# Linear attention, gated convolution and channel mixing on one core: heating transposes, query and first weights put in another order

## The chip, the cores and the metric

The kernel runs on one core of a Trainium2 chip. Times are device microseconds (us) of one execution; the number compared is the median of several runs. One execution was taken with the hardware profiler, and all rows below are from it. Of the engines, PE is TensorE, PEld its weight load, DVE VectorE, ACT ScalarE, POOL GpSimd, and SP issues most transfers.

## The reference

Three layers follow each other on batch 8, sequence 576, width 512 (8 heads of 64); the weights come as 64-bit numbers, q, k and v as 32-bit ones.

```python
# attention: softmax of q over the head's width, of k over the sequence
q_s = exp(q - max(q, -1)); q_s /= sum(q_s, -1) + 1e-9
k_s = exp(k - max(k, 2));  k_s /= sum(k_s, 2) + 1e-9
x = q_s @ (k_s^T @ v)                       # per batch and head, heads put side by side
# gated convolution
gate = sigmoid(sum_t conv_w[t] * x shifted by 4 - t)      # 5 taps, per channel
x = (gate * (x @ w_val)) @ w_out
# channel mixing, x_prev = x one step earlier
xk = mu_k * x + (1 - mu_k) * x_prev;  xr = mu_r * x + (1 - mu_r) * x_prev
out = sigmoid(xr @ w_r) * (relu(xk @ w_k) ** 2 @ w_v)     # w_k 512x1024, w_v 1024x512
```

## The kernel before, in words

The 4608 tokens are worked in 12 tiles of 384. Each tile goes through the same steps: query's softmax (qexp, qnorm), its transposes (xturn: tile pq) and copies (xq: tile q), the product with the attention matrix (x: tile px, copied to xf), the gate (taps on DVE at L705, tanh on ACT at L714), the product with W_val (V: pv), gf = gate times pv, the product with W_out (Y: py), mixing with the token before (y, mixk: yf and xm), then W_r (R: racc), W_k (H: ph) and W_v (A: vacc).

The attention matrix of a batch is made in rounds of 4 heads from k and v. A round takes k's maximum over the sequence: DVE over the steps (tile pm), PE turns it (pmT, L359), DVE takes the maximum m (L362), PE spreads it (mx, L405), DVE subtracts it from k (L406), ACT takes the exponential (L409), PE multiplies with v (kvacc, L419), and DVE divides (kvf, L431). Query's first tile comes in two halves of 4 heads, tile came, each with its own maximum, exponential (L492) and division (L503).

Weights come as 64-bit numbers (tile raw) and are decoded to 32 bits (tile whole) by ACT and DVE (L165 to L178). Raw weights pass through six buffers; five of them (LEFT_WEIGHTS: wval1, wr0, wk1, wk2, wk5) share a single seventh one, so that each of their loads waits for the decode of the one before. The transfers stand in SP's queue one behind another.

`heat` (L925) is a group of 8 transposes of the identity into a bank that nobody reads.

Three things set the order. FRONT, a table of step names, is the order in which the steps of the first tiles are written; up to the step START a scheduler may then move instructions. `after(key)` says that an instruction is to stand behind another one, named by `latest`. BEHIND does the same for the decoding of a weight: ("mus", "m1.0") puts its part on ACT behind the step that left mus, and its part on DVE behind the maximum of round 0.

Of the kernel before, what the change touches and what calls it, by code (L numbers as in the profile page):

```python
# [77 lines left out]
def tile_linear_attention_gated_conv_channel_mix(  # L78
# [61 lines left out]
    def f32(ap):  # L140
        return ap.bitcast(F32)
# [212 lines left out]
    def kv_turn(st):  # L354
        pm, n, x = st["pm"], HR * D // P, rounds.index(st)
        pmT = bank_of(st, "pmT", 1)
        with after("matmul" if x > 1 else None):
            for j in range(n):
                nc.tensor.transpose(pmT[:, j * P:(j + 1) * P], pm[:, j * P:(j + 1) * P], f32(ident))  # L359
        m1 = odd.tile([P, n], F32, tag="m1", bufs=2, name="m1")  # L360
        with after("kvf.0" if x == 1 else None):
            latest[f"m1.{x}"] = nc.vector.tensor_reduce(  # L362
                out=m1, in_=pmT[:, :n * P].rearrange("p (j t) -> p j t", j=n), axis=AX.X, op=ALU.max
            )
        st["m1"] = m1
# [45 lines left out]
    def kv_mm(st):  # L411
# [4 lines left out]
        for x in range(n):  # L416
            for s in range(NST):
                for e in range(2):
                    nc.tensor.matmul(  # L419
                        acc[e * D:(e + 1) * D, x * VW:(x + 1) * VW], lhsT=kt[:, 2 * x + e, s, :],  # L420
                        rhs=st["v"][:, 2 * x + e, s, :], start=(s == 0), stop=(s == NST - 1),
                    )
# [185 lines left out]
    def x_turn(st, i, c):  # L608
        qt = st["qt"]
        pq = ps_t.tile([P, 512], F32, tag="t", name="pq")  # L610
        for t in range(NT):
            nc.tensor.transpose(  # L612
                pq[:, t * P:(t + 1) * P], qt[:, t, 2 * c:2 * c + 2, :].rearrange("p h d -> p (h d)"), f32(ident)
            )
        st["pq", c] = pq
# [75 lines left out]
    def x_gate(st, i, c):  # L691
# [10 lines left out]
        with after("kexp.1" if i == 0 and c == 0 else None):  # L702
            nc.scalar.activation(gx(gate), data, AF.Copy, scale=tap(c, HALO))  # L703
        for sh in range(1, NTAP):
            latest[f"tap.{sh}"] = nc.vector.scalar_tensor_tensor(  # L705
                out=gx(gate), in0=xv[:, :, HALO - sh:HALO - sh + L], scalar=tap(c, HALO - sh),
                in1=gx(gate), op0=ALU.mult, op1=ALU.add,
            )
# [11 lines left out]
    def main_steps(i, xs):  # L720
# [63 lines left out]
        def keep_y(c, py):  # L784
            yv = padded(i, 1, "yf", 4, "yf")
            fill_past(i, yv, tail_y[:, c:c + 1])
            latest["yf"] = nc.scalar.activation(yv[:, :, 1:], gx(py[:, :T]), AF.Copy, scale=0.5 if i == 0 else 1.0)
            keep_tail(i, yv, tail_y[:, c:c + 1])
            st["yv", c] = yv
            mix(c, "xr", mur, omr, "x", x_pair)  # L790

        def mix(c, key, mu, om, tag, pair):
            yv = st["yv", c]
            xf = one(tag, 8, "xm") if i == 0 else scratch("xm")
            nc.scalar.activation(gx(xf), yv[:, :, 0:L], AF.Copy, scale=om[:, c:c + 1])  # L795
# [129 lines left out]
    def heat():  # L925

        po = ps_acc.tile([P, 512], F32, tag="acc", name="heat")
        for x in range(8):
            nc.tensor.transpose(po[:, x % 4 * P:(x % 4 + 1) * P], f32(ident), f32(ident))  # L929
# [76 lines left out]
```

## Time and profile before

| | |
|---|---|
| median of 3 runs | 802.05 us (801.37 to 802.36) |
| profiled execution, its own time | 801.24 us |
| its span from first to last instruction | 799.4 us |
| PE busy, PEld busy | 782.9 us (98%), 688.6 us (86%) |
| DVE busy, ACT busy | 598.2 us (75%), 481.9 us (60%) |
| mean granted clock of PE | 0.994 |
| W_k's loads, 512 KB each | 8, median 3.2 us from issue to landing |

The shares are of the whole span. In slices of 20 us (40 of them) PE is busy 5 tenths of the first one and 8 of the second, and 9 or more from then on; the granted clock is 8 tenths in the first and 9 in the others. So the page alone says little about the front, and the rows below are from views with narrow windows there. A duration is that of one instruction from its start to its modelled end; matmuls overlap, so two starts tell more of the pace than one duration. In the timeline one fp32 matmul of a product is counted twice (x2), a transpose once.

### The profile page before, as it was taken

How to read it: one execution, taken by the hardware profiler on the slowest of the kernel's cores; microseconds unless marked ns; L12 is line 12 of the kernel's file. 1: busy time of each engine (PE TensorE's matmuls, PEld its weight loads, DVE VectorE, ACT ScalarE, POOL GpSimd, SP SyncE). 2: the span in 40 equal slices, each digit the busy share in tenths (PEclk: the TensorE clock that was granted, in tenths of full speed). 3: DMA queues.
4: the chain of work that ended last, by engine and by line, in shares of the span. 5: the costliest groups of instructions: out<-in, count | busy, mean ns of one | idle time of the engine just before them, and what ended most of it. 6: DMA issues, size and time to landing. Idle time of an engine off the chain costs nothing.

```text
span 799.4 us, 12507 instructions
## 1 busy us (share of the span) xinstructions
PE 782.9 (98%) x4426; PEld 688.6 (86%) x4426; DVE 598.2 (75%) x1182; ACT 481.9 (60%) x977; POOL 64.4 (8%) x224
## 2 busy tenths in 40 slices
PE   5899999999999999999999999999999999999998
PEld 5545569989989999999999999999999998998996
DVE  5799879988788588687888768768878857755511
ACT  3678477745763763763773773673674665574542
POOL 2012010100001110100010200100000100110000
PEclk8999999999999999999999999999999999999999
DMA  9788220033332412411531501502513112110001
GB/s 324 203 247 276 64 80 1 6 102 104 82 100 75 111 40 67 119 40 53 140 90 57 139 25 62 139 5 80 137 44 108 57 30 69 57 36 28 12 1 40
DMA packets 91709, 68.89 MB, mean 86 GB/s; under 512 B 48738, under 2 KB 83454, under 8 KB 91646
## 3 DMA queue, kind: packets, MB, share of 16 engines
q1 hardware_dynamic: 91600, 68.06, 28.5%
q8 instruction: 35, 0.57, 0.3%
q14 instruction: 28, 0.23, 0.1%
q10 hardware_dynamic: 46, 0.02, 0.0%
HBM read 51.54 MB, written 16.53 MB: 85 GB/s over the span
## 4 chain that ended last, share of the span: by engine, by line
PE 90%; DVE 4%; DMA 2%; ACT 2%; issue 1%; DVEq 0%; ACTq 0%
PE vacc L585 24%; PE ph L585 24%; PE py L585 12%; PE pv L585 11%; PE racc L585 11%; PE px L585 3%; PE kvacc L419 2%; DVE whole L176 1%; DMA raw<-in_moe_w_k_dram 1%; DMA raw<-in_moe_w_v_dram 1%; PE heat L929 1%; DMA kt<-in_k_dram 1%; ACT raw L169 1%; DVE gate L705 1%; PE pq L612 1%
## 5 line engine op out<-in xcount | busy, mean ns | idle before, releaser
L705 DVE SCALAR_TENSOR_TENSOR gate<-xf,cw,gate 128x384 f32<-128x384 f32 x192 | 116.7, 615 | 5.7 <-ACT gate L703 2.4
L585 PE MATMUL ph<-xkh,wk_hi 128*128 128x384 f32 x352 | 118.5, 337 | 0.0
L585 PE MATMUL ph<-xkl,wk_hi 128*128 128x384 f32 x352 | 118.2, 336 | 0.0
L585 PE MATMUL ph<-xkh,lower 128*128 128x384 f32 x352 | 117.8, 336 | 0.0
L822 ACT ACTIVATE rf<-ph 128x384 f32<-128x384 f32 x96 | 46.9, 489 | 96.2 <-PE ph L585 95.8
L578 DVE TENSOR_TENSOR kl<-rf,kh 128x384 fp32r<-128x384 f32 x88 | 49.0, 556 | 74.5 <-ACT kh L577 74.2
L585 PE MATMUL vacc<-wv_hi,kh 128*128 128x512 f32 x264 | 103.9, 394 | 0.0
L585 PE MATMUL vacc<-lower,kh 128*128 128x512 f32 x264 | 103.4, 392 | 0.0
L585 PE MATMUL vacc<-wv_hi,kl 128*128 128x512 f32 x264 | 103.2, 392 | 0.0
L577 ACT CAST gh<-gf 128x384 fp32r<-128x384 f32 x44 | 22.6, 513 | 104.2 <-DVE gf L757 104.2
L585 PEld LDWEIGHTS ph<-xkh,wk_hi 128*128 128x128 f32 x352 | 66.1, 188 | 2.4 <-ACT xkh L577 0.2
L585 PEld LDWEIGHTS ph<-xkh,lower 128*128 128x128 f32 x352 | 66.1, 188 | 2.3
L585 PEld LDWEIGHTS ph<-xkl,wk_hi 128*128 128x128 f32 x352 | 66.1, 188 | 0.0
L796 DVE SCALAR_TENSOR_TENSOR xm<-yf,mus,xm 128x384 f32<-128x384 f32 x96 | 56.1, 612 | 12.8 <-ACT xm L795 12.5
L585 PE MATMUL py<-gh,wout_hi 128*128 128x384 f32 x176 | 60.0, 341 | 0.0
L585 PE MATMUL pv<-xh,wval_hi 128*128 128x384 f32 x176 | 59.3, 337 | 0.0
L585 PE MATMUL py<-gl,wout_hi 128*128 128x384 f32 x176 | 58.9, 337 | 0.0
L585 PE MATMUL pv<-xl,wval_hi 128*128 128x384 f32 x176 | 58.9, 335 | 0.0
L585 PE MATMUL pv<-xh,lower 128*128 128x384 f32 x176 | 58.9, 334 | 0.0
L585 PEld LDWEIGHTS vacc<-wv_hi,kl 128*128 128x128 f32 x264 | 49.5, 188 | 10.8 <-DVE kl L578 0.3
L585 PE MATMUL py<-gh,lower 128*128 128x384 f32 x176 | 58.8, 336 | 0.0
L795 ACT ACTIVATE xm<-yf,mus 128x384 f32<-128x384 f32 x96 | 56.4, 615 | 3.0 <-DVE xrl L578 1.6
(153 smaller groups left out, 1703.1 us busy)
## 6 DMA issues: line engine op xcount, KB each, us to landing
out_dram<-rs SPq DMA_DIRECT2D x36, 256.0 KB, 2.3
kt<-in_k_dram SPq DMA_DIRECT2D x16, 512.0 KB, 4.3
vt<-in_v_dram SPq DMA_DIRECT2D x56, 128.0 KB, 4.0
turned<-sq SPq DMA_DIRECT2D x36, 192.0 KB, 2.1
qT<-turned SPq DMA_DIRECT2D x72, 96.0 KB, 2.2
qn<-in_q_dram SPq DMA_DIRECT2D x24, 192.0 KB, 3.5
raw<-in_moe_w_k_dram SPq DMA_DIRECT2D x8, 512.0 KB, 3.2
raw<-in_moe_w_v_dram SPq DMA_DIRECT2D x8, 512.0 KB, 3.3
```

What stands on the lines that cost most here:

```text
L169: nc.scalar.activation(f32(high), f32(high), AF.Prelu, scale=2.0 ** -112, alpha=2.0 ** 32)
L176: return nc.vector.scalar_tensor_tensor(out=out.bitcast(U32), in0=high, scalar=3, in1=low, op0=ALU.logical_shift_left, op1=ALU.bitwise_or)
L419: nc.tensor.matmul(acc[e * D:(e + 1) * D, x * VW:(x + 1) * VW], lhsT=kt[:, 2 * x + e, s, :], rhs=st["v"][:, 2 * x + e, s, :], start=(s == ...
L577: latest["round"] = nc.scalar.copy(pair[0], a)
L578: latest["split"] = nc.vector.tensor_sub(pair[1], a, f32(pair[0]))
L585: latest["matmul"] = nc.tensor.matmul(po, lhsT=left[a], rhs=right[b], start=start and x == 0, stop=stop and x == len(m) - 1)
L612: nc.tensor.transpose(pq[:, t * P:(t + 1) * P], qt[:, t, 2 * c:2 * c + 2, :].rearrange("p h d -> p (h d)"), f32(ident))
L705: latest[f"tap.{sh}"] = nc.vector.scalar_tensor_tensor(out=gx(gate), in0=xv[:, :, HALO - sh:HALO - sh + L], scalar=tap(c, HALO - sh), in1= ...
L795: nc.scalar.activation(gx(xf), yv[:, :, 0:L], AF.Copy, scale=om[:, c:c + 1])
L796: latest["mix"] = nc.vector.scalar_tensor_tensor(out=gx(xf), in0=yv[:, :, 1:], scalar=mu[:, c:c + 1], in1=gx(xf), op0=ALU.mult, op1=ALU.add)
L822: nc.scalar.activation(rf, ph[:, :T], AF.Relu)
L929: nc.tensor.transpose(po[:, x % 4 * P:(x % 4 + 1) * P], f32(ident), f32(ident))
```

## The change

The table FRONT is written anew: heat6 and heat3 stand ahead of mm0 (the first kvacc), heat0 behind xturn1.0, heat7 is gone, and turn1 (the second pmT) stands behind query's first two turns. New places for `after`: the first kvacc behind the heats; the second pmT behind the heats; a group of heats behind pq of chunk 1 once that is there; in the first tile, ACT's part of gate 1 behind the exponential of query's second half, and the gates' third and fourth taps behind the division of it (qmul). The decoding of wval2 and wval3 on DVE goes behind that division (before: behind kvf of round 1), and that of wk0, wk1, wv0 and wv1 behind the mixing steps (before: wv0 alone, and its part on ACT behind yf).

```diff
@@ -22,10 +22,10 @@
 
 FRONT = (
     "qload.0 qload0.0 lk0 cload consts lwval0 lv0 lk1 lwval1 lv1 lwval2 qload1.0 lwval3 lwout0 lwout1 lwr0 max0 turn0 "
-    "exp0 lwout3 lwr1 heat1 heat2 lwout2 qexp0.0 wval0 vcopy0 mm0 heat6 qnorm0.0 heat3 heat0 heat7 max1 turn1 xturn0.0 "
-    "xq0.0 xturn1.0 xq1.0 x0.0 exp1 wval1 x1.0 vcopy1 others qexp1.0 V0.0 mm1 qnorm1.0 gate0.0 V1.0 xturn2.0 xq2.0 "
+    "exp0 lwout3 lwr1 heat1 heat2 lwout2 qexp0.0 wval0 vcopy0 heat6 heat3 mm0 qnorm0.0 max1 xturn0.0 xq0.0 xturn1.0 "
+    "xq1.0 heat0 turn1 x0.0 exp1 wval1 x1.0 vcopy1 others qexp1.0 V0.0 mm1 qnorm1.0 gate0.0 V1.0 xturn2.0 xq2.0 "
     "x2.0 wval2 wval3 V2.0 xturn3.0 xq3.0 x3.0 gate1.0 gate2.0 V3.0 lwr2 wout0 gf0.0 gf1.0 gate3.0 gf2.0 lwk1 gf3.0 "
-    "lwk2 lwr3 wout1 lwk0 wout2 wout3 Y0.0 wr0 Y1.0 wr1 Y2.0 wr2 Y3.0 lwv1 y0.0 wk1 y1.0 max2 y2.0 y3.0 lwv0 wk0 lwk3 "
+    "lwk2 lwr3 wout1 lwk0 wout2 wout3 Y0.0 wr0 Y1.0 wr1 Y2.0 wr2 Y3.0 lwv1 y0.0 y1.0 max2 y2.0 y3.0 wk1 lwv0 wk0 lwk3 "
     "lwk5 R0.0 R1.0 lwk4 lwk7 wr3 mixk0.0 lwk6 mixk1.0 R2.0 mixk2.0 R3.0 mixk3.0 wk3 wk2 turn2 exp2 lwv2 qload.1 H0.0 "
     "wv1 lwv5 H1.0 H2.0 wk4 lwv4 wv0 mm2 wk5 rsig.0 A0.0 lwv3 H3.0 wk6 wv5 max3 A1.0 wk7 H4.0 wv2 qexp.1 turn3 exp3 "
     "A2.0 wv3 H5.0 lwv6 lwv7 mm3 qnorm.1 xturn0.1 xq0.1 wv7 A3.0 wv4 H6.0 x0.1 xturn1.1 xq1.1 gate0.1 A4.0 x1.1 "
@@ -65,10 +65,10 @@
 
 ON_SCALAR = "wval0 wval1 wval2 wval3 wout0 wout1 wout2 wout3".split()
 BEHIND = {
-    "wval0": ("mus", "m1.0"), "wval1": ("kexp.0", "m1.1"), "wval2": ("qexp.1", "kvf.1"), "wval3": ("qexp.1", "kvf.1"),
+    "wval0": ("mus", "m1.0"), "wval1": ("kexp.0", "m1.1"), "wval2": ("qexp.1", "qmul"), "wval3": ("qexp.1", "qmul"),
     "wout0": ("xf.3", "kvf.1"), "wout1": ("xf.3", "kvf.1"), "wout2": ("xf.3", "gf.1"), "wout3": ("xf.3", "gf.1"),
     "wr0": ("tanh", "gf.1"), "wr1": ("tanh", "gf.1"), "wr2": ("tanh", "gf.1"), "wr3": ("tanh", "gf.1"),
-    "wv0": ("yf", "mix"),
+    "wk0": ("part", "mix"), "wk1": ("part", "mix"), "wv0": ("part", "mix"), "wv1": ("part", "mix"),
 }
 
 LEFT_WEIGHTS = "wval1 wr0 wk1 wk2 wk5".split()
@@ -354,7 +354,7 @@
     def kv_turn(st):
         pm, n, x = st["pm"], HR * D // P, rounds.index(st)
         pmT = bank_of(st, "pmT", 1)
-        with after("matmul" if x > 1 else None):
+        with after((None, "heat", "matmul", "matmul")[x] if x < 4 else "matmul"):
             for j in range(n):
                 nc.tensor.transpose(pmT[:, j * P:(j + 1) * P], pm[:, j * P:(j + 1) * P], f32(ident))
         m1 = odd.tile([P, n], F32, tag="m1", bufs=2, name="m1")
@@ -416,10 +416,11 @@
         for x in range(n):
             for s in range(NST):
                 for e in range(2):
-                    nc.tensor.matmul(
-                        acc[e * D:(e + 1) * D, x * VW:(x + 1) * VW], lhsT=kt[:, 2 * x + e, s, :],
-                        rhs=st["v"][:, 2 * x + e, s, :], start=(s == 0), stop=(s == NST - 1),
-                    )
+                    with after("heat" if st is rounds[0] and x + s + e == 0 else None):
+                        nc.tensor.matmul(
+                            acc[e * D:(e + 1) * D, x * VW:(x + 1) * VW], lhsT=kt[:, 2 * x + e, s, :],
+                            rhs=st["v"][:, 2 * x + e, s, :], start=(s == 0), stop=(s == NST - 1),
+                        )
         sums = acc[:, 0:n * VW].rearrange("p (j c) -> p j c", c=VW)
         den = odd.tile([P, n], F32, tag="den", bufs=2, name="den")
         d3 = den.rearrange("p (j o) -> p j o", o=1)
@@ -609,7 +610,7 @@
         qt = st["qt"]
         pq = ps_t.tile([P, 512], F32, tag="t", name="pq")
         for t in range(NT):
-            nc.tensor.transpose(
+            latest[f"pq.{c}"] = nc.tensor.transpose(
                 pq[:, t * P:(t + 1) * P], qt[:, t, 2 * c:2 * c + 2, :].rearrange("p h d -> p (h d)"), f32(ident)
             )
         st["pq", c] = pq
@@ -699,13 +700,14 @@
         if i == 0 and c in CONV_ON_TENSOR:
             nc.scalar.activation(gate, conv_on_tensor(xv, c), AF.Tanh, scale=0.5)
             return
-        with after("kexp.1" if i == 0 and c == 0 else None):
+        with after(("kexp.1", "qexp.1", None, None)[c] if i == 0 else None):
             nc.scalar.activation(gx(gate), data, AF.Copy, scale=tap(c, HALO))
         for sh in range(1, NTAP):
-            latest[f"tap.{sh}"] = nc.vector.scalar_tensor_tensor(
-                out=gx(gate), in0=xv[:, :, HALO - sh:HALO - sh + L], scalar=tap(c, HALO - sh),
-                in1=gx(gate), op0=ALU.mult, op1=ALU.add,
-            )
+            with after("qmul" if i == 0 and sh > 2 else None):
+                latest[f"tap.{sh}"] = nc.vector.scalar_tensor_tensor(
+                    out=gx(gate), in0=xv[:, :, HALO - sh:HALO - sh + L], scalar=tap(c, HALO - sh),
+                    in1=gx(gate), op0=ALU.mult, op1=ALU.add,
+                )
         if i < LATER or c < 2:
             x_tanh(st, c)
 
@@ -784,7 +786,7 @@
         def keep_y(c, py):
             yv = padded(i, 1, "yf", 4, "yf")
             fill_past(i, yv, tail_y[:, c:c + 1])
-            latest["yf"] = nc.scalar.activation(yv[:, :, 1:], gx(py[:, :T]), AF.Copy, scale=0.5 if i == 0 else 1.0)
+            nc.scalar.activation(yv[:, :, 1:], gx(py[:, :T]), AF.Copy, scale=0.5 if i == 0 else 1.0)
             keep_tail(i, yv, tail_y[:, c:c + 1])
             st["yv", c] = yv
             mix(c, "xr", mur, omr, "x", x_pair)
@@ -792,7 +794,7 @@
         def mix(c, key, mu, om, tag, pair):
             yv = st["yv", c]
             xf = one(tag, 8, "xm") if i == 0 else scratch("xm")
-            nc.scalar.activation(gx(xf), yv[:, :, 0:L], AF.Copy, scale=om[:, c:c + 1])
+            latest["part"] = nc.scalar.activation(gx(xf), yv[:, :, 0:L], AF.Copy, scale=om[:, c:c + 1])
             latest["mix"] = nc.vector.scalar_tensor_tensor(
                 out=gx(xf), in0=yv[:, :, 1:], scalar=mu[:, c:c + 1], in1=gx(xf), op0=ALU.mult, op1=ALU.add
             )
@@ -926,7 +928,8 @@
 
         po = ps_acc.tile([P, 512], F32, tag="acc", name="heat")
         for x in range(8):
-            nc.tensor.transpose(po[:, x % 4 * P:(x % 4 + 1) * P], f32(ident), f32(ident))
+            with after("pq.1" if "pq.1" in latest and x == 0 else None):
+                latest["heat"] = nc.tensor.transpose(po[:, x % 4 * P:(x % 4 + 1) * P], f32(ident), f32(ident))
 
     acts = [{} for _ in range(NB + 1)]
     todo_front = {"cload": load_consts, "consts": turn_consts, "others": other_consts, "kvsplit": kv_split}
```

PE's instructions, from the heats ahead of the first pmT to the first pv. Before:

```order
L929 MATMUL heat<-ident 128x128 x14
L359 MATMUL pmT<-ident,pm 128x128 x2
L405 MATMUL mx<-ident,m_187 128x128 x2
L419 MATMUL kvacc<-vt,kt 64x65 x20
L929 MATMUL heat<-ident 128x128 x32
L359 MATMUL pmT<-ident,pm 128x128 x2
L612 MATMUL pq<-ident,qt 128x128 x6
L585 MATMUL px<-q,kvf_118 128x384
L405 MATMUL mx<-ident,m_302 128x128 x2
L585 MATMUL px<-q,kvf_118 128x384
L585 MATMUL pv<-xf,whole 128x384 x4
```

The same place on PE now:

```order
L932 MATMUL heat<-ident 128x128 x15
L359 MATMUL pmT<-ident,pm 128x128 x2
L932 MATMUL heat<-ident 128x128 x5
L405 MATMUL mx<-ident,m_187 128x128 x2
L932 MATMUL heat<-ident 128x128 x10
L420 MATMUL kvacc<-vt,kt 64x65 x20
L613 MATMUL pq<-ident,qt 128x128 x6
L932 MATMUL heat<-ident 128x128 x8
L359 MATMUL pmT<-ident,pm 128x128 x2
L586 MATMUL px<-q,kvf_118 128x384
L405 MATMUL mx<-ident,m_305 128x128 x2
```

Of the 32 heats behind the first kvacc 16 stand ahead of it, 8 are gone, and 8 stand behind pq, which came behind all of them.

DVE's instructions from query's second half less its maximum (qt<-came,qm) to the division of it (qt<-qt,qs). Before:

```order
L491 TENSOR_TENSOR qt<-came,qm 128x3x256
L705 SCALAR_TENSOR_TENSOR gate<-xf,cw,gate 128x384 x3
L426 TENSOR_SCALAR den<-kvacc 128x2
L500 TENSOR_REDUCE qs<-qt 128x12
L427 RECIPROCAL den<-den 128x2
L705 SCALAR_TENSOR_TENSOR gate<-xf,cw,gate 128x384
L431 TENSOR_TENSOR kvf_118<-kvacc,den 64x2x64 x2
L501 TENSOR_SCALAR qs<-qs 128x12
L705 SCALAR_TENSOR_TENSOR gate<-xf,cw,gate 128x384
L502 RECIPROCAL qs<-qs 128x12
L176 SCALAR_TENSOR_TENSOR whole<-raw 128x512
L503 TENSOR_TENSOR qt<-qt,qs 128x3x256
```

The same place on DVE now, and what stands behind it:

```order
L492 TENSOR_TENSOR qt<-came,qm 128x3x256
L707 SCALAR_TENSOR_TENSOR gate<-xf,cw,gate 128x384 x2
L501 TENSOR_REDUCE qs<-qt 128x12
L427 TENSOR_SCALAR den<-kvacc 128x2
L502 TENSOR_SCALAR qs<-qs 128x12
L428 RECIPROCAL den<-den 128x2
L503 RECIPROCAL qs<-qs 128x12
L432 TENSOR_TENSOR kvf_118<-kvacc,den 64x2x64 x2
L504 TENSOR_TENSOR qt<-qt,qs 128x3x256
L707 SCALAR_TENSOR_TENSOR gate<-xf,cw,gate 128x384
L176 SCALAR_TENSOR_TENSOR whole<-raw 128x512
L707 SCALAR_TENSOR_TENSOR gate<-xf,cw,gate 128x384
```

Three gate taps and the decode of wval2 moved from ahead of the division to behind it; the two taps that stay are of gate 0.

ACT's instructions at the mixing, from the last decodes ahead of the first yf on. Before:

```order
L169 ACTIVATE raw<-raw 128x512 x6
L787 ACTIVATE yf<-py 128x384
L795 ACTIVATE xm<-yf,mus 128x384
L787 ACTIVATE yf<-py 128x384 x2
L169 ACTIVATE raw<-raw 128x512
L795 ACTIVATE xm<-yf,mus 128x384 x2
L787 ACTIVATE yf<-py 128x384
L795 ACTIVATE xm<-yf,mus 128x384 x5
L169 ACTIVATE raw<-raw 128x512 x5
```

Now:

```order
L169 ACTIVATE raw<-raw 128x512 x4
L789 ACTIVATE yf<-py 128x384
L797 ACTIVATE xm<-yf,mus 128x384
L789 ACTIVATE yf<-py 128x384 x2
L797 ACTIVATE xm<-yf,mus 128x384 x2
L789 ACTIVATE yf<-py 128x384
L797 ACTIVATE xm<-yf,mus 128x384 x2
L169 ACTIVATE raw<-raw 128x512 x2
L797 ACTIVATE xm<-yf,mus 128x384 x3
```

Two decodes (wk0, wv1) ahead of the first yf and one (wk1) behind the third moved behind the mixing of xr; on DVE the decode of wk1, which stood behind the first xm, stands behind the fifth. Also on ACT, the tanh of gate 0, which stood ahead of the copies of the second pair of pq, stands between these and the copies of px.

## Rows read from the trace of the kernel before

**Rows 1.** Windows: span, busy us (instructions) of PE, PEld, DVE, ACT, POOL, clock, DMA, GB/s.

```profile
56.00:87.00 31.00, 30.60 (x122) 15.84 (x121) 29.36 (x54) 25.48 (x47) 7.20 (x10) 1.00 0.68 211
92.90:799.40 706.50, 702.99 (x4028) 639.87 (x4026) 522.10 (x1040) 420.83 (x869) 50.56 (x176) 1.00 0.23 68
```

**Rows 2.** Timeline of PE, front: start, us, engine, line, op, shapes, count, [idle before, releaser].

```profile
13.37 2.44 PE L419 MATMUL kvacc<-vt,kt 128*64 128x65 f32 x40 [2.93 <-ACT kt L409]
15.73 5.50 PE L929 MATMUL heat<-ident 128*128 128x128 f32 x32
21.07 0.38 PE L359 MATMUL pmT<-ident,pm 128*128 128x128 f32 x2
21.29 0.82 PE L612 MATMUL pq<-ident,qt 128*128 128x128 f32 x6
22.34 0.91 PE L585 MATMUL px<-q,kvf 128*128 128x384 f32 x2 [0.24 <-ACT q L624]
...
26.63 1.39 PE L419 MATMUL kvacc<-vt,kt 128*64 128x65 f32 x40
```

**Rows 3.** Timeline of DVE, front and mixing.

```profile
13.79 0.96 DVE L503 TENSOR_TENSOR qt<-qt,qs 128x768 f32<-128x768 f32 x1
...
16.50 0.59 DVE L431 TENSOR_TENSOR kvf<-kvacc,den 64x128 f32<-64x128 f32 x2
21.49 0.42 DVE L362 TENSOR_REDUCE m<-pmT 128x2 f32<-128x256 f32 x1 [4.40 <-PE pmT L359]
...
23.51 1.49 DVE L406 TENSOR_TENSOR kt<-kt,mx 128x1280 f32<-128x1280 f32 x1 [0.88 <-PE mx L405]
...
26.98 1.68 DVE L705 SCALAR_TENSOR_TENSOR gate<-xf,cw,gate 128x384 f32<-128x384 f32 x3
...
31.43 0.63 DVE L176 SCALAR_TENSOR_TENSOR whole<-raw 128x512 uint32<-128x512 uint32 x1
31.98 0.94 DVE L503 TENSOR_TENSOR qt<-qt,qs 128x768 f32<-128x768 f32 x1
...
54.53 0.69 DVE L176 SCALAR_TENSOR_TENSOR whole<-raw 128x512 uint32<-128x512 uint32 x1 [0.36 <-ACT raw L169]
```

**Rows 4.** Windows again, for the granted clock (third number from the end).

```profile
13.50:14.00 0.50, 0.50 (x12) 0.50 (x14) 0.47 (x3) 0.50 (x2) 0.00 (x0) 0.50 1.12 317
20.00:21.00 1.00, 1.00 (x12) 1.00 (x11) 0.00 (x0) 0.00 (x0) 0.00 (x0) 1.00 0.85 340
52.40:56.50 4.10, 2.79 (x7) 1.13 (x7) 3.02 (x6) 3.63 (x9) 0.83 (x3) 1.00 1.03 359
```

**Rows 5.** Timeline of PE in two short windows inside the 32 heats.

```profile
16.64 0.85 PE L929 MATMUL heat<-ident 128*128 128x128 f32 x3
...
20.30 0.82 PE L929 MATMUL heat<-ident 128*128 128x128 f32 x6
```

**Rows 6.** Timeline of PE from the second pq on.

```profile
33.07 1.51 PE L612 MATMUL pq<-ident,qt 128*128 128x128 f32 x6 [2.27 <-DVE qt L503]
...
36.87 5.32 PE L585 MATMUL pv<-xf,whole 128*128 128x384 f32 x16
42.03 10.48 PE L585 MATMUL py<-gf,whole 128*128 128x384 f32 x32
53.28 1.98 PE L585 MATMUL racc<-whole,xm 128*128 128x512 f32 x4 [0.76 <-DVE xm L796]
55.80 8.85 PE L585 MATMUL racc<-whole,xm 128*128 128x512 f32 x20 [0.55 <-DVE xm L796]
...
87.40 0.43 PE L405 MATMUL mx<-ident,m 128*128 128x128 f32 x2 [0.80 <-DVE m L362]
```

**Rows 7.** Timeline of ACT, copies behind the second pq and px.

```profile
33.97 0.48 ACT L624 COPY q<-pq 128x384 f32<-128x384 f32 x1 [2.04 <-PE pq L612]
...
36.19 0.48 ACT L657 COPY xf<-px 128x384 f32<-128x384 f32 x1 [1.09 <-PE px L585]
```

**Rows 8.** The chain that ended last, in order of time: start, us, what.

```profile
49.59 6.56 DMA raw<-in_moe_w_k_dram
```

## Prediction

> **What bounds the kernel now.** I read the windows first. From 92.9 us to the end TensorE is busy for 702.99 of 706.50 us [rows 1]: nothing the change touches lies there, and the end moves only by how much earlier TensorE comes to that point. So I read TensorE's timeline up to it, looking at three things: idle time in brackets, matmuls that feed nothing (tile heat), and matmuls that run at half pace.
>
> The front [rows 2]: TensorE idles 2.93 us (from 10.44) until the exponential for the first kvacc is there, runs that kvacc in 2.44 us where the second one, at 26.63, takes 1.39, then issues 32 heating transposes in 5.34 us (15.73 to 21.07), and only behind them pmT, pq and px. These 32 are not idle filling: the row of VectorE's maximum m shows it waiting 4.40 us for pmT, which stands behind them, while its inputs were there [rows 3]. The granted clock says why the kvacc is slow: 0.50 at 13.5 (the 1.2 GHz level), 1.00 from 20 us on [rows 4]. The heats show it too: three at 16.64 span 0.85 us, 0.21 from one to the next, six at 20.30 span 0.82, 0.11 from one to the next [rows 5].
>
> Later [rows 6]: 2.27 us of idle before the second pq, since VectorE's division of query's second half ends at 32.92 [rows 3]; pq and px after it at half pace; 0.76 and 0.55 before racc; 0.80 before an mx. After both long idle pieces (2.93 and 2.27) the clock was at its lower level; after the pieces of 0.76 and 0.55 it stayed at 1.00 [rows 4].
>
> **The change part by part**, on the profiled execution's own time, 801.24 us (0.81 under the median of the three runs, 802.05; I take the same offset afterwards).
>
> *Heats.* Before, 48 transposes; now 40: one less group of 8, 16 of the 32 in front of the first kvacc, 8 left behind it. Where do the 16 fall? One more ahead of the first pmT, into the wait for pm; 5 between pmT and mx, into the wait for VectorE's m; 10 between mx and kvacc: at 0.11 each they end near 11.5, at 0.21 near 12.5, both before 13.37, when the exponential releases kvacc. So they cost nothing; their cover is the exponential's chain, and without it 16 would cost 1.8 to 3.4 us. Should the 5 run at 0.21, mx comes 0.3 later, and so would kvacc; I take 0, 0.3 is the bound.
>
> Now the order after kvacc, pq, 8 heats, pmT, px [rows 2]: kvacc 13.37 + 1.39 = 14.76 if the clock holds. pq needs qt, divided by 14.75 [rows 3], and takes 0.82: 15.58. Heats 8 x 0.11: 16.46. pmT to the next issue 0.22: 16.68. px also needs kvf; VectorE ended it at 17.09, 1.36 after kvacc's last issue [rows 3], now about 16.1; and q, two copies of 0.48 behind pq [rows 7], 16.6. So px at 16.7 where it stood at 22.34: **5.65 us**. The same shift holds for VectorE's subtraction kt (23.51 to about 17.9), and with it the exponential and the second kvacc: mx comes within 0.7 of pmT.
>
> *Query's second half ahead of gates and weights.* From that subtraction to the end of the division VectorE takes 32.92 - 23.51 = 9.41 us [rows 3]. Out of that stretch go three of five gate taps at about 0.54 (three start to end in 1.68) and one decode of 0.6; the two taps left belong to one gate, so the second waits for the first: about 0.3 back. That leaves 7.5: the division ends at 17.9 + 7.5 = 25.4, and pq follows at 25.45 instead of 33.07: 7.62 earlier, **1.97 more**. TensorE's work before it ends at 30.80 - 5.65 = 25.15, so the idle shrinks from 2.27 to 0.3.
>
> *Pace behind it.* pq and px ran 33.07 to 36.87, 3.80 us, at half pace [rows 6]. After 0.3 us of idle I expect full pace: first pq 0.4, copy 0.48, px 0.8, copy 0.48, and in between a loss that is new: on ScalarE the tanh of gate 0 (taken as long as a copy) now stands ahead of the copies of px and waits for two taps and a decode that VectorE does after the division (25.4 + 0.54 + 0.6 + 0.65 = 27.2) [rows 3, 7]. So pv's second half at 28.15, 2.70 behind pq: **1.10 more**. From 27.2 VectorE has eleven taps at about 0.58, five decodes at 0.6, one shift of a third of a microsecond and gf's four products (as long as a tap) to do, some 12 us: gf's last is there near 39.3, while py, behind 5.16 us of pv, starts at 33.3 and comes to its fourth row at 41.2. So pv and py (36.87 to 52.5, 15.6 us [rows 6]) follow without a wait and end at 43.8.
>
> *W_k's and W_v's first weights behind the mixing.* On ScalarE a decode of W_v stood ahead of the first yf and one of W_k between yf and xm; both are now behind. The second racc wait (0.55) goes and the first (0.76) loses about 0.4: **0.95**. The price is that wk1 is decoded later against the rest, and one buffer passes wval1, wr0, wk1, wk2, wk5 along, each load waiting for the decode of the one before. wk1 was whole at 55.22, 2.7 behind py's end [rows 3, 6], behind one mixing step on VectorE; now five stand ahead of it, 4 x 0.54 more: 4.9 behind 43.8, 48.7. wk2's load then takes 3.2 us, the page's median for W_k's loads, up to 6.56, which one shows with others beside it [rows 8]; with 1.3 for its shift and decode it is whole at 53.2 to 56.6. ph starts behind racc's 10.8 us, at 44.2 + 10.8 = 55.0 [rows 6], and asks for wk2 0.6 later, so it may wait 0 to 1 us; I take 0 (nearer to the median), and 0.25 for the mx that now stands behind that decode on VectorE. What is late next: the mx that waited 0.80, which I put at 0.5. Net **0.05**.
>
> Sum: 5.65 + 1.97 + 1.10 + 0.95 + 0.05 = 9.7 us; 801.24 - 9.7 = 791.5, on the median's scale **792.4 us**.
>
> *A rule against this.* Transposes did bring the clock back here: from 15.73 to 21.07 TensorE ran only heats, and their spacing went from 0.21 to 0.11 while the grant went to 1.00 [rows 2, 4, 5]. The Trainium skill, TensorE: Matmul & The Clock Gate, Part 4: PE-mode transpose, says that the full clock does not engage for transposes, which do not count as busy in the same way. By that rule the heats moved in front of kvacc would hold nothing, and the result would be the first rival below; the trace disagrees as to raising the clock, and does not show whether heats hold it.
>
> **Rivals.**
> 1. *The heats don't hold the clock.* The longest idle piece falls from 2.93 to about 1.8 us, between 0.76 (held) and 2.27 (lost) [rows 4, 6], so the rows leave it open. Then kvacc takes 2.44, pq 6 x 0.21 = 1.28, heats 1.70, pmT 0.43: px at 19.2, 2.5 later; 794.9.
> 2. *VectorE and the loads take it back.* For it: in that stretch the chain that ended last runs through loads and decodes, not through TensorE [rows 8]. Against: before, TensorE waited for none of them there, busy for 30.60 of 31.00 us from 56 to 87 us [rows 1]. If only VectorE's lead at the subtraction (5.6) and the 0.4 of racc survive: 6.0, 796.0.
> 3. *Slower: the lower clock stays.* The fall that now comes at 33 us comes early and outlasts the second block's waits. Price: pv's second half and py, 36.87 to 52.5 [rows 6], are 15.6 us at full pace and as much again at half; 801.24 - 9.7 + 15.6 = 807.1, on the median's scale 808. It decides from 9.7 us of full-pace work run at half pace on; before, the grant came back within 4 us of steady work, which speaks against.
> 4. *The heats only move the wait.* pmT would have to be late for another reason than heats; VectorE's pm stands ahead of kvf, which ended at 17.09 [rows 3], so hardly: no change, 802.
>
> **How the numbers follow.** Forecast 0.56 (its own range 791 to 794), rival 1 0.22, rival 2 0.14, rival 3 0.04, rival 4 0.04. The first three are faster by over 0.2% (1.6 us, about what a measurement of this kernel can tell from no change): 0.92; within 0.2% 0.04; slower 0.04. The range goes from 790.5 (the last racc and mx waits gone as well, about 1.5) to 797.2, which takes in rivals 1 and 2.
>
> **What would show it.** Right: kvacc at 13.4 lasting 1.4 with a grant of 1.00; px near 16.7; the second pq near 25.5 with under 1 us of idle; pv's second half near 28; racc near 44 with one wait; the pq that stood at 92.9, behind the fourth kvacc, near 83. Wrong: a grant of 0.50 between 12.5 and 28; ph waiting for a decode or a load near 55; waits at mx over 1 us near 57 or 77; kvacc released later than 13.4.

## The result, and the profile after

| | before | after |
|---|---|---|
| median | 802.20 us (801.37 to 802.40, 4 runs) | 791.01 us (790.05 to 791.73, 4 runs) |
| ratio, 95% interval | | 0.9862 [0.9845, 0.9879] |
| profiled execution, its own time | 801.24 us | 790.96 us |
| span | 799.4 us | 789.2 us |

Faster by 11.2 us in the medians and by 10.3 in the two profiled executions; forecast were 792.4 us and a gain of 9.7. The timeline of PE after (start, us, engine, line, operation, count, [idle before, releaser]):

```profile
10.72 0.64 PE L405 MATMUL mx<-ident,m 128*128 128x128 f32 x2
11.14 1.35 PE L932 MATMUL heat<-ident 128*128 128x128 f32 x10
14.29 1.39 PE L420 MATMUL kvacc<-vt,kt 128*64 128x65 f32 x40 [1.79 <-ACT kt L409]
...
17.58 0.81 PE L586 MATMUL px<-q,kvf 128*128 128x384 f32 x2
...
26.49 0.85 PE L613 MATMUL pq<-ident,qt 128*128 128x128 f32 x6 [0.47 <-DVE qt L504]
...
29.05 5.43 PE L586 MATMUL pv<-xf,whole 128*128 128x384 f32 x16
...
55.40 0.38 PE L359 MATMUL pmT<-ident,pm 128*128 128x128 f32 x2
...
76.57 0.43 PE L405 MATMUL mx<-ident,m 128*128 128x128 f32 x2
...
82.55 0.55 PE L613 MATMUL pq<-ident,qt 128*128 128x128 f32 x3
```

Of before, beside [rows 2, 6], its first mx, its fourth kvacc and the pq behind that:

```profile
10.01 0.43 PE L405 MATMUL mx<-ident,m 128*128 128x128 f32 x2 [0.52 <-DVE m L362]
...
91.55 1.39 PE L419 MATMUL kvacc<-vt,kt 128*64 128x65 f32 x40 [0.27 <-ACT kt L409]
92.86 0.55 PE L612 MATMUL pq<-ident,qt 128*128 128x128 f32 x3
```

Against these rows: kvacc takes 1.39 us for 2.44. Its 20 products are issued 1.8 us behind the last heat instead of 2.93 behind mx. px stands at 17.58 for 22.34 (4.76 earlier), the second pq at 26.49 for 33.07 (6.58), pv's second half at 29.05 for 36.87 (7.82), pmT behind racc at 55.40 for 64.49 (9.09), and the pq that stood at 92.86 at 82.55: 10.31, the whole gain of the profiled execution. Only kvacc's start is later than before, 14.29 for 13.37.

From there to the end nothing was gained or lost, as the windows show (span, busy us and instructions of PE, PEld, DVE, ACT, POOL, granted clock, DMA share, GB/s); they answer to [rows 1, 4]:

```profile
56.00:87.00 31.00, 31.00 (x166) 17.43 (x165) 29.44 (x52) 23.59 (x42) 0.61 (x2) 1.00 0.63 186
82.55:789.20 706.65, 703.06 (x4030) 640.06 (x4026) 524.89 (x1044) 421.20 (x871) 50.43 (x176) 1.00 0.23 68
14.30:15.70 1.40, 1.37 (x40) 1.23 (x40) 1.37 (x4) 1.11 (x2) 0.00 (x0) 1.00 1.03 342
27.50:30.00 2.50, 2.43 (x7) 1.36 (x8) 2.43 (x5) 2.20 (x6) 0.37 (x2) 1.00 0.55 172
```

PE is busy in all 31 us from 56 to 87, and the grant reads 1.00 in kvacc and behind the second pq, where it had read 0.50. For the place behind the second pq, before (span, busy us and instructions of PE, granted clock, DMA share, GB/s):

```profile
33.50:34.00 0.50, 0.50 (x5) 0.50 0.96 295
```

DVE after, to be read against [rows 3]: the second round's maximum waits 0.57 us for pmT instead of 4.40, and from the subtraction (18.85) to the end of the division (26.34) it takes 7.49 us where it took 9.41.

```profile
9.89 0.42 DVE L362 TENSOR_REDUCE m<-pmT 128x2 f32<-128x256 f32 x1 [0.83 <-PE pmT L359]
...
17.78 0.42 DVE L362 TENSOR_REDUCE m<-pmT 128x2 f32<-128x256 f32 x1 [0.57 <-PE pmT L359]
...
18.85 1.48 DVE L406 TENSOR_TENSOR kt<-kt,mx 128x1280 f32<-128x1280 f32 x1
...
25.38 0.96 DVE L504 TENSOR_TENSOR qt<-qt,qs 128x768 f32<-128x768 f32 x1
...
55.06 1.29 DVE L176 SCALAR_TENSOR_TENSOR whole<-raw 128x512 uint32<-128x512 uint32 x2 [0.64 <-ACT raw L169]
```

### The profile page after: what moved, and what is told of

Its sections match the earlier page's. It is cut to its first block, busy times and chain, and to the rows that moved or that the text cites. A ratio compares the mean times of both kernels' runs of the same rounds, so it can differ in the third digit from the quotient of the medians.

```text
span 789.2 us, 12489 instructions
## 1 busy us (share of the span) xinstructions
PE 777.9 (99%) x4418; PEld 685.2 (87%) x4418; DVE 598.3 (76%) x1182; ACT 481.6 (61%) x977; POOL 61.7 (8%) x224
## 4 chain that ended last, share of the span: by engine, by line
PE 96%; DVE 2%; issue 1%; DMA 0%; ACT 0%; ACTq 0%; DVEq 0%
PE ph L586 26%; PE vacc L586 26%; PE racc L586 13%; PE pv L586 12%; PE py L586 12%; PE px L586 3%; PE kvacc L420 3%; PE heat L932 1%; PE pq L613 1%; DVE gate L707 1%; DMA mut<-in_moe_mu_r_dram 0%; DVE whole L176 0%; DVE kt L406 0%; PE pmT L359 0%; ACT kt L409 0%
```

## Experiments

All medians, each with that of the kernel before on the same chip. The intervals are 0.0013 to 0.0019 to either side, 1.0 to 1.5 us, so smaller differences between two rows are not settled by them.

| kernel | median us | before beside it | lower by | ratio, 95% interval |
|---|---|---|---|---|
| after (second, third group) | 790.53, 790.82 | 801.04, 800.99 | 10.5, 10.2 | 0.9873 [0.9859, 0.9886], 0.9869 [0.9850, 0.9888] |
| A no heats in front of kvacc | 793.16 | 801.06 | 7.9 | 0.9905 [0.9891, 0.9918] |
| B before, without its 32 heats | 794.31 | 801.06 | 6.75 | 0.9921 [0.9907, 0.9935] |
| C heats alone | 797.39 | 801.04 | 3.65 | 0.9952 [0.9939, 0.9965] |
| D heats and wk1's place | 794.59 | 800.99 | 6.4 | 0.9916 [0.9898, 0.9935] |
| E query's part undone | 795.27 | 801.06 | 5.8 | 0.9923 [0.9909, 0.9938] |
| F as E, heats before the second pq | 795.01 | 800.99 | 6.0 | 0.9923 [0.9905, 0.9940] |
| G weights' part undone | 792.60 | 801.06 | 8.5 | 0.9893 [0.9878, 0.9909] |
| H no heats behind pq | 792.35 | 801.04 | 8.7 | 0.9898 [0.9883, 0.9913] |
| I as H, all 16 heats behind mx | 792.42 | 801.04 | 8.6 | 0.9895 [0.9882, 0.9909] |
| J as H, DVE's order held | 791.14 | 800.99 | 9.9 | 0.9877 [0.9859, 0.9895] |

### The kernel after, twice more

No edit. What was expected:

> The changed kernel once more, unaltered, so that the others of this group have it beside them on their chip and the start of the first kvacc can be read from a second profile. Theory (the 0.92 by which kvacc came later in the first profile, 14.29 for 13.37, is how that one execution's transfers landed): kvacc at 13.4 to 14.0 with mx within 0.4 of 10.01; ratio to the kernel before 0.986. Rival (the five heats between pmT and mx put it back every time): kvacc again at 14.2 or later, mx at 10.6 or later, same ratio.

> The changed kernel once more, unaltered, beside the others of this group. Theory: kvacc's start between 13.2 and 14.3 as the first loads land, everything behind it as in its other profiles (second pq 12.2 behind kvacc, no wait over 0.6 behind it), ratio 0.986 to 0.988. Rival (the earlier two profiles were lucky): a wait of over 1 us at mx or ph in this one.

PE in the first of the two:

```profile
5.90 3.24 PE L932 MATMUL heat<-ident 128*128 128x128 f32 x15
...
9.23 0.71 PE L932 MATMUL heat<-ident 128*128 128x128 f32 x5
...
13.27 1.39 PE L420 MATMUL kvacc<-vt,kt 128*64 128x65 f32 x40 [1.84 <-ACT kt L409]
...
16.61 0.81 PE L586 MATMUL px<-q,kvf 128*128 128x384 f32 x2
...
25.51 0.85 PE L613 MATMUL pq<-ident,qt 128*128 128x128 f32 x6 [0.47 <-DVE qt L504]
...
28.08 5.43 PE L586 MATMUL pv<-xf,whole 128*128 128x384 f32 x16
...
44.01 10.57 PE L586 MATMUL racc<-whole,xm 128*128 128x512 f32 x24 [0.18 <-DVE xm L798]
54.42 0.38 PE L359 MATMUL pmT<-ident,pm 128*128 128x128 f32 x2
...
76.09 0.43 PE L405 MATMUL mx<-ident,m 128*128 128x128 f32 x2 [0.42 <-DVE m L362]
...
82.07 0.55 PE L613 MATMUL pq<-ident,qt 128*128 128x128 f32 x3
```

This execution starts like the profiled one of before (kvacc at 13.27 for 13.37), and each step stands within 0.1 us of the forecast: px 16.61 (16.7), pq 25.51 (25.45), pv 28.08 (28.15). In the second one the five heats between pmT and mx span 1.27 us instead of 0.71, mx starts at 10.94 and kvacc at 14.51, over the 14.3 expected of it. So the same program starts kvacc at 13.27, 14.29 and 14.51. In every profile but one (I) it starts 2.93 or 2.94 us behind the end of mx, so the late start arises ahead of that: PE is still at half pace up to mx. In the first profile of after mx ends 1.05 us behind m (10.31 to 11.36), in that of before and in the repeat with the early start 0.49. Not all of these 0.56 us are the heats': in A, B and I below, with no heat between pmT and mx and PE at half pace, mx ends 0.75 behind m. The five heats at half pace cost 0.30 (1.05 - 0.75), the bound of the forecast, and mx's own half pace 0.26. The remaining 0.36 of the 0.92 by which kvacc came later is m, which ended at 10.31 instead of 9.95.

### A. No heats in front of kvacc

```diff
-    "... wval0 vcopy0 heat6 heat3 mm0 qnorm0.0 ..."
+    "... wval0 vcopy0 mm0 qnorm0.0 ..."
```

> The changed kernel without the two groups of heats in front of the first kvacc (24 heats are left, 16 of them at the start and 8 behind pq); PE's order is otherwise the same. Theory (the heats hold the clock): PE idles about 3.3 us between mx and kvacc, the grant is 0.50 from about 12.6, kvacc takes 2.44 us as before the change, pq 1.3, the 8 heats 1.7, so px comes near 19.6 and the later work of the front 2 us later than in the changed kernel (px 17.58): 793.0 us, 792.4 to 794.5. Rival (the clock falls or stays for another reason than these heats): kvacc takes 1.39 as in the changed kernel, released 0.3 earlier since mx no longer stands behind 5 heats: 790.7 us. Second rival (the fall costs nothing, since VectorE's chain sets the second pq): the grant falls, but the second pq stays within 0.5 us of 26.5: 791.2.

PE, and below it m on DVE and a window inside kvacc:

```profile
10.34 0.69 PE L405 MATMUL mx<-ident,m 128*128 128x128 f32 x2 [0.52 <-DMA kt<-in_k_dram]
13.96 2.44 PE L420 MATMUL kvacc<-vt,kt 128*64 128x65 f32 x40 [2.93 <-ACT kt L409]
...
18.91 0.81 PE L586 MATMUL px<-q,kvf 128*128 128x384 f32 x2
```

```profile
9.86 0.42 DVE L362 TENSOR_REDUCE m<-pmT 128x2 f32<-128x256 f32 x1 [0.86 <-PE pmT L359]
```

```profile
14.00:15.00 1.00, 1.00 (x20) 1.00 (x21) 0.97 (x3) 1.00 (x2) 0.00 (x0) 1.00 0.93 316
```

The time came as the theory had it: without the heats the wait is 2.93 us again, kvacc takes 2.44 again and px stands 4.95 behind kvacc's start, with them 3.29 and 3.34. 793.16 us where 793.0 was expected: 7.9 below the kernel before beside it, and the kernel after is 10.2 to 11.2 below. But the clock did not fall here. The two transposes of mx took 0.69 us (0.43 before the change), so PE was at half pace already when the idle time began, and the grant, which reads 1.00 inside this slow kvacc too (20 instructions counted in that microsecond; 40 in 1.40 us in the kernel after), shows no change. B is the same in both. So A shows that kvacc runs at full pace with the heats and at half pace without them, not that a clock once up is lost over 2.93 us; that only the kernel before shows.

### B. The kernel before, without its 32 heats

```diff
-    "... vcopy0 mm0 heat6 qnorm0.0 heat3 heat0 heat7 max1 ..."
+    "... vcopy0 mm0 qnorm0.0 max1 ..."
```

> The kernel before, with the 32 heats behind the first kvacc taken out and nothing else changed. Theory (they were on the path, and steady work alone brings the clock back): kvacc as before 2.44 us at half pace, px about 4.7 us earlier than 22.34, the second pq 4.5 earlier than 33.07, the waits there and later as before: 797.3 us. Rival (the heats were what brought the clock back): pv, the second kvacc and px run at half pace up to the second pq, some 4 us more, and all but 1 us of it is lost: 800.5. Against both: another wait of the front holds pmT, and the time stays at 802.

```profile
14.32 2.44 PE L419 MATMUL kvacc<-vt,kt 128*64 128x65 f32 x40 [2.93 <-ACT kt L409]
...
18.02 0.39 PE L359 MATMUL pmT<-ident,pm 128*128 128x128 f32 x2
18.24 0.83 PE L585 MATMUL px<-q,kvf 128*128 128x384 f32 x2
...
29.06 0.84 PE L612 MATMUL pq<-ident,qt 128*128 128x128 f32 x6 [2.38 <-DVE qt L503]
30.15 1.56 PE L585 MATMUL px<-q,kvf 128*128 128x384 f32 x4 [0.24 <-ACT q L624]
```

Both numbers expected were too high: 794.31 us. The heats were not needed to bring the clock back, since kvacc and pq did it (pmT in 0.39 us, pv right behind at full pace). px came 4.10 earlier although kvacc started 0.95 later (4.7 expected). At the second pq the lead is still 4.01. Behind it 2.38 us of idle stand much as before (2.27), but this time pq and px ran at full pace (1.56 us for px), and pv's second half stands 5.24 earlier: 1.23 more. Another 0.65 came by the pmT behind racc, and 1.07 more because neither the fourth mx nor the fourth kvacc waited. So more than half of what the whole change gains can be had by deleting 32 instructions.

### C and D. Heats alone, and heats with wk1's place

C undoes both other parts (the edits of E and G together). D is C with this line of the change, and wk1 in the table where the change has it:

```diff
-    "wv0": ("yf", "mix"),
+    "wk1": ("part", "mix"), "wv0": ("yf", "mix"),
```

> The changed kernel with both other parts undone: only the heats and the second pmT stand in their new places. Theory (the terms of the sum hold one by one): px 3.3 us behind kvacc's start, the second pq near 28.5 after 2.3 us of idle, waits of 0.6 to 0.8 before racc: 5.65 us below the kernel before, 796.3 on its scale, and up to 2.4 less in executions in which the clock holds over that idle piece. Rival A (the parts overlap; the waits that the other parts take away would have gone anyway with the earlier front): 793 or less. Rival B (heats in front of kvacc matter little; taking 32 heats off the path alone gave 794.3): 794.3 as well, within 0.5.

> The kernel with the heats alone, and of the other two parts only one weight's place: wk1 behind the mixing (its place in the table too); wk0, wv0 and wv1 as before the change, query's part undone. Theory (in the kernel with the heats alone VectorE stood 2.42 us at wk1's shift ahead of the first mixing step, for a load that had not landed, and the wait of 2.25 us before racc and the fall of the clock in racc came from that): no wait over 0.9 before racc, racc in 10.6 us: 3.3 us below the kernel with the heats alone (797.4), 794.1. Rival (the late load is met elsewhere, by ACT or at ph): the wait shows again at ph or mx, 796 to 797.

C, DVE at the mixing and PE:

```profile
48.90 0.43 DVE L175 TENSOR_SCALAR raw<-raw 128x512 uint32<-128x512 uint32 x1 [2.42 <-DMA raw<-in_moe_w_k_dram]
```

```profile
28.93 2.61 PE L586 MATMUL px<-q,kvf 128*128 128x384 f32 x4 [0.24 <-ACT q L625]
...
49.90 12.18 PE L586 MATMUL racc<-whole,xm 128*128 128x512 f32 x24 [2.25 <-DVE xm L798]
```

D, PE at the same place:

```profile
47.87 10.57 PE L586 MATMUL racc<-whole,xm 128*128 128x512 f32 x24 [0.31 <-DVE xm L798]
```

In C the front comes earlier (px 3.30 behind kvacc) but W_k's load does not: wk1's shift stands ahead of the first mixing step on DVE and waits 2.42 us for it, racc waits 2.25, the grant is 0.50 from 50 to 53 us, and racc takes 1.61 more. One weight moved behind the mixing takes away all of that: 0.31 and 10.57, and the median falls by 2.8 (3.3 expected). So in the kernel with the heats alone this single place in the order is worth about three times the 0.95 that the forecast gave to the whole part. The part's other places add nothing that the medians show: D has wk1's alone (6.4 below before), E below has all of them (5.8).

### E and F. Query's part undone, and its idle time heated

```diff
-    "wval2": ("qexp.1", "qmul"), "wval3": ("qexp.1", "qmul"),
+    "wval2": ("qexp.1", "kvf.1"), "wval3": ("qexp.1", "kvf.1"),
-        with after(("kexp.1", "qexp.1", None, None)[c] if i == 0 else None):
+        with after("kexp.1" if i == 0 and c == 0 else None):
-            with after("qmul" if i == 0 and sh > 2 else None):
+            with after(None):
```

F adds two groups of heats behind the last product of V1, in a bank of another pool:

```diff
-    "... gate0.0 V1.0 xturn2.0 ..."
+    "... gate0.0 V1.0 heat7 heat5 xturn2.0 ..."
```

> The changed kernel with the part on query's second half undone: ACT's part of gate 1, the third and fourth taps and the decoding of wval2 and wval3 stand as they stood before; PE's order is the same. Theory (taps and decode ahead of the division cost 1.97 us, and the longer idle piece then costs the clock): the second pq at 28.4 after about 2.3 us of idle, the grant 0.50 behind it, pv's second half about 3 us later than 29.05: 794.0 us. Rival A (the delay counts, the clock holds because it was only lost through the earlier fall): 793.0. Rival B (the lead of the front is swallowed by gf or the mixing anyway): 791.3.

> The changed kernel with the part on query's second half undone, as before, and 16 heats behind the first half of pv, in the idle time before the second pq. Theory (of the 4.3 us that undoing cost, 1.9 are the delay and the rest the clock): the second pq as late as without these heats, about 28.5, but pq and px at full pace, grant 1.00 from 26 to 34: 793.1. Rival A (the clock costs nothing, the whole is the delay and a later wait at mx): 795.3 as without them. Rival B (the heats end behind the division and put pq back): the second pq 0.3 or more later, 795.5 or more.

PE in E, then in F:

```profile
28.59 1.16 PE L613 MATMUL pq<-ident,qt 128*128 128x128 f32 x6 [2.38 <-DVE qt L504]
29.67 2.89 PE L586 MATMUL px<-q,kvf 128*128 128x384 f32 x4
...
81.36 0.43 PE L405 MATMUL mx<-ident,m 128*128 128x128 f32 x2 [1.66 <-DVE m L362]
```

```profile
28.14 0.85 PE L613 MATMUL pq<-ident,qt 128*128 128x128 f32 x6 [0.65 <-DVE qt L504]
29.23 1.56 PE L586 MATMUL px<-q,kvf 128*128 128x384 f32 x4 [0.24 <-ACT q L625]
```

Counted from kvacc's start (14.47 in E, 14.01 in F), pq comes at 14.12 and 14.13 in these two and at 12.20 in the kernel after: the delay is 1.92 us (forecast 1.97). pv's second half comes at 17.93 in E, 16.70 in F, 14.76 in the kernel after: 1.23 is the clock's. The five executions of E point the same way: four at 794.96 to 795.80 with a mean clock of 0.998, one at 793.13 with 1.000. The medians of E and F do not: 795.27 and 795.01, where 794.0 and 793.1 were expected, with F's six executions from 793.83 to 796.39. The profiles are of E's slowest execution (795.80) and of F's fastest (793.83), so the 1.2 us are there in those two and do not show as a gain in F's median. In F's three slowest executions the mean clock reads 0.998 or 0.999, in the others 1.000; that the clock fell in them in spite of the heats would fit, but no profile shows it. Undone, the part costs 4.4 to 4.7 us in the time and not the 3.07 forecast; 1.66 of it is the wait at the fourth mx.

### G. Weights' part undone

```diff
-    "wk0": ("part", "mix"), "wk1": ("part", "mix"), "wv0": ("part", "mix"), "wv1": ("part", "mix"),
+    "wv0": ("yf", "mix"),
-    "... lwv1 y0.0 y1.0 max2 y2.0 y3.0 wk1 lwv0 ..."
+    "... lwv1 y0.0 wk1 y1.0 max2 y2.0 y3.0 lwv0 ..."
```

> The changed kernel with the part on W_k's and W_v's first weights undone: wk0, wk1 and wv1 have no place behind the mixing, wv0 has its place of before, and wk1 stands behind y0. Theory A (this part also took away the 0.80 of an mx and the 0.27 of a kvacc later on, by what it moved on VectorE): two waits before racc, 0.76 and 0.55, and about 1 us of waits at mx and kvacc near 77 and 80: 793.2 us. Theory B (these later waits went for another reason, such as the earlier front): the two racc waits alone come back: 792.1. Theory C (the racc waits came from elsewhere too): 791.0.

```profile
44.63 10.57 PE L586 MATMUL racc<-whole,xm 128*128 128x512 f32 x24 [0.65 <-DVE xm L798]
...
56.51 0.43 PE L405 MATMUL mx<-ident,m 128*128 128x128 f32 x2 [0.44 <-DVE m L362]
```

792.60 us lies between B (792.1) and A (793.2), and the profile (the fastest of its four executions) fits neither: one racc wait came back instead of two, and a wait at the third round's mx instead of the fourth's. The part is worth about 2 us against 10.2 to 10.5, where the forecast had 1.0.

### H, I and J. Fewer heats, heats elsewhere, the order held

The planner named here is the scheduler that may move the instructions of the first tiles. H drops heat0 from the table and puts the second pmT behind pq. I puts both groups in front of kvacc behind mx besides. J is H with

```diff
-    "wk0": ("part", "mix"), "wk1": ("part", "mix"), "wv0": ("part", "mix"), "wv1": ("part", "mix"),
+    "wk0": ("part", "mix"), "wk1": ("part", "mix"), "wv0": ("part", "m1.2"), "wv1": ("part", "mix"),
+    "wk3": (None, "mix"), "wk4": (None, "m1.2"), "wk5": (None, "m1.2"), "wk6": (None, "m1.2"), "wk7": (None, "m1.2"),
```

> The changed kernel without the 8 heats behind pq; the second pmT stands right behind pq. Theory (kvf, ended at 17.2 in the profile of the changed kernel, releases px next): px at 17.25 for 17.58 at the same start of kvacc, kept to the end: 0.3 us below the changed kernel beside it. Rival A (all of their 0.87 us is won): 0.9 below. Rival B (these heats hold the clock over the wait for kvf): a grant or pace of half from 17 us on, second pq and pv later, 1 us or more above the changed kernel.

> As the kernel without the 8 heats behind pq, and the 16 heats in front of kvacc all stand behind mx, none between pmT and mx. Theory (half-pace heats put mx back): mx right behind m, 10.0 to 10.4, kvacc 0.3 to 0.7 us earlier than with the heats ahead of mx, full pace in kvacc: 0.6 to 1.0 below the changed kernel. Rival A (k's loads or VectorE set mx anyway): no earlier, equal to the kernel without the 8 heats. Rival B (without heats between pmT and mx the clock is still low at mx's end, and 16 heats at half pace end behind the exponential): kvacc 0.3 later and 0.3 above it.

> The changed kernel without the 8 heats behind pq, and with VectorE's order ahead of the third round's maximum held by hand: the decoding of wk3 behind the mixing, that of wk4 to wk7 and wv0 behind that maximum, where the planner had put two of them ahead of it. Theory (the 1.8 us by which the kernel without these heats came out above the changed one are the decodes that the planner then put ahead of the maximum, not the heats): no wait at mx near 57, px 0.3 earlier at the same start of kvacc, and all of it kept: 790.2, or 0.3 below the changed kernel beside it. Rival A (the heats themselves did it, or some other order of the planner): a wait of over 1 us at mx or later, 792 again. Rival B (pinning five decodes later makes ph wait for wk2 to wk5): ph waits near 58 to 65, 791 to 793.

H, DVE and PE near 57:

```profile
54.97 2.49 DVE L176 SCALAR_TENSOR_TENSOR whole<-raw 128x512 uint32<-128x512 uint32 x4
```

```profile
57.84 0.43 PE L405 MATMUL mx<-ident,m 128*128 128x128 f32 x2 [1.53 <-DVE m L362]
```

I, PE:

```profile
10.94 3.52 PE L932 MATMUL heat<-ident 128*128 128x128 f32 x16
14.39 1.39 PE L420 MATMUL kvacc<-vt,kt 128*64 128x65 f32 x40
```

J, PE, and DVE up to the fourth round's maximum in a window:

```profile
55.27 0.43 PE L406 MATMUL mx<-ident,m 128*128 128x128 f32 x2
...
76.74 0.43 PE L406 MATMUL mx<-ident,m 128*128 128x128 f32 x2 [1.03 <-DVE m L363]
```

```profile
66.00:76.00 10.00, 9.94 (x20) 1.00 0.76 219
```

In H px came 0.26 earlier from kvacc's start and everything up to pmT 0.38, as the theory had it, and then 1.53 us were lost at mx: 792.35, a miss in sign. The planner had moved: eight heats fewer on PE, and it put four decodes ahead of the third maximum on DVE where it had put two (x4 in the row above, x2 at 55.06 in the kernel after). J puts them back and the wait near 57 is gone, which shows that it was this order and not the heats. But J is no faster than the kernel after beside it (791.14 for 790.82): it waits 1.03 at the fourth round's mx, and the 0.3 expected of it did not come. In I the heats at half pace took 3.52 us and released kvacc themselves, its rival B (by mx, which ended at 11.15, kvacc would have started at 14.08); it waits at the third mx as H does, 1.17 us.

The fourth mx tells what limits the front now. Kvacc starts at 13.27, 14.29 and 14.51 in the three executions of after and at 13.61 in J, but that mx at 76.09, 76.57, 76.78 and 76.74. A spread of 1.24 us has shrunk to 0.69. DVE is busy for 9.94 of 10 us ahead of it, in J and in the first profile of after alike. It gets to that maximum when the work in front of it there (decodes, and the softmax of the next tile's query) lets it, and a front that is earlier by a few tenths waits: 0.42 us in the repeat that started earliest, none in the other two. No kernel tried is faster than the changed one.

## Why the prediction was right, and where not

*Heats ahead of kvacc, 5.65.* Right, 5.73 in the execution with an equal start (22.34 to 16.61), by the order of steps given: kvacc at full pace, then pq, eight heats, pmT. kvacc runs at full pace behind the heats: in the ten profiles with them and an idle piece of 1.60 to 1.84 us it took 1.39; in the three without (before, A, B) 2.93 us of idle went ahead of 2.44. The forecast had the heats hold a clock that is up. That is so in seven of the ten, where mx ran at full pace (0.38 or 0.43 us) and 1.84 us of idle followed the heats. In the other three (both after with a late start, and E) mx still ran at half pace (0.63 or 0.64), and the pace came up in the ten heats behind it (1.35 us for ten in the first of them, where the half pace of I would make 2.3). Whether it is the heats' work or the shorter idle time that keeps the pace was not separated, since the heats bring both. The cost of the moved heats was put at 0 with a bound of 0.3; it is 0 or 0.30, as the five heats between pmT and mx run. One of the signs named for being wrong did come, a kvacc released later than 13.4, in two of three executions of after; it cost little, 790.96 and 791.15 us for 790.48, since what stands behind kvacc moved as forecast and the fourth mx took back part of the difference.

*The rule weighed there.* The Trainium skill, TensorE: Matmul & The Clock Gate, Part 4: PE-mode transpose, says that the full clock does not engage for transposes. The trace disagrees. The rows weighed in the prediction could not settle it, since a kvacc ran ahead of those heats and B comes back to full pace without them. The openings settle it: up to the first kvacc PE runs nothing but transposes. In the first repeat of after five heats at 9.23 span 0.71 us where five at half pace span 1.27, and in I a kvacc at full pace stands right behind 16 heats.

*Query's half ahead, 1.97, and full pace behind it, 1.10.* Right: 1.83 and 1.23 between those steps of the equal start (7.56 - 5.73, 8.79 - 7.56), and 1.92 and 1.23 from E against the profiles of after and F.

*Racc's waits, 0.95.* From pv to the pmT behind racc the lead grew by 1.28 (10.07 - 8.79): the waits of 0.76 and 0.55 left 0.18, not 0.4. That is 1.13; the rest is that the products in between ran 0.15 shorter.

*Net 0.05 for what is late next.* This is the mis-sized term, 0.72 (10.79 - 10.07). Neither the loss at the third round's mx came (0.25 charged, none measured; wk2 was whole in time and ph did not wait) nor did a wait of 0.5 at the fourth: 0, 0.42 and 0 in three executions. A wait of 0.3 before the fourth kvacc, which the forecast did not have, went as well.

*Additivity.* The sum was right, stage by stage in the whole kernel, but its terms are not what each part is worth by itself. Worked out from the table, the heats alone gave 3.65 and not 5.65. Query's part is worth 4.4 to 4.7 taken out of the whole (E) and 4.8 put on top of the heats (G less C), not 3.07; W_k's and W_v's 1.7 to 2.0 taken out (G) and 2.1 put on top (E less C), not 1.0. For these two parts the two ways agree within the intervals. No kernel has them without the heats, so what the heats are worth taken out of the whole is not known; A takes out 16 of them, for 2.3 to 2.6. With the front early and one of the others missing, a wait that was hidden before (the load of wk1, the idle time before pq and the clock behind it, the fourth mx) takes part of the lead back. Rival 2, that VectorE and the loads take it back, is what happened in C, and D shows which instruction it hangs on; in the whole change that instruction had been moved.

*Rivals.* Rival 1 has its price in kernel A: 793.16, where 794.9 was worked out. At px the lower clock cost 1.6 us (4.95 behind kvacc for 3.29 or 3.34) and not 2.5, since PE was back at full pace at pmT; in the time A stands 2.2 to 2.6 above the kernel after. Most of what is left to 794.9 is that the whole change came out 1.4 below its own forecast. Rivals 3 and 4 did not come.

## What to carry to other kernels

Price an edit in the order in which its stages wait, and ask of each stage that comes earlier which load or decode now stands ahead of it on its engine: a lead is kept only where the whole chain moves. Measure what one part of a change gives, alone or taken out of the whole, and do not read it off its term in the sum; here the two differ by about 1 to 2 us. Where a planner sets the order, any instruction dropped can move others 40 us later, so compare its order before the times.

## What was not expected of the hardware

The recorded grant is not the pace. In A and B it reads 1.00 through a kvacc of 2.44 us, which runs at half pace; in before it read 0.50 there, with the same 2.44. From 6 to 8 us it reads 1.00 in all fourteen profiles, although the first heats stand 0.22 us apart there, which is half pace. The Trainium skill, TensorE: Matmul & The Clock Gate, Part 1: The HAM clock gate, warns that such records have been seen to be unreliable on this chip; the traces of A and B agree. The spacing of equal matmuls is the safer reading.

An idle piece of nearly one length does not always cost the clock: behind 2.38 us before the second pq (PE at full pace ahead of it in all four), px took 2.89 us in E, 2.61 in C, 2.20 in D, where the pace fell sooner or later, and 1.56 in B, where it did not fall.
